# Stage three of a fused attention, gMLP and gated-attention kernel: PSUM handed out by two pools, two moved groups of work, a split gate step and a one-engine last copy

## The chip, the cores and the metric

One core of a Trainium2 chip runs the whole program. The metric is the device time of one execution in microseconds; the kernel before was timed three times. One more execution was taken by the hardware profiler, and all rows below are from that one. TensorE is PE in the rows (its weight loads PEld), VectorE is DVE, ScalarE is ACT, GpSimd is POOL, and SyncE, which issues the transfers, is SP.

## The reference

Four batches of 576 tokens with 512 features go through three stages. Stage one is a pooled plus a local attention, stage two a gMLP block. Stage three, the only one that the change touches, is a mixture of four attention experts with a causal mask, weighted per token by the two largest of four gate logits:

```python
logits = x @ w_gate
topk = np.argpartition(-logits, K, axis=-1)[..., :K]
for e in range(E):
    q = x @ wq[e]; k = x @ wk[e]; v = x @ wv[e]
    scores = np.where(causal, -1e9, scale * (q @ k.transpose(0, 2, 1)))
    a = softmax(scores)
    out += gate_weight[e] * (a @ v @ wo[e])
```

## The kernel before

Stage three works in a fixed order that the program writes out itself; nothing is rescheduled later. Every matmul input of the projections is held as a high and a low part (`split`, L198: ACT copies the high part, DVE subtracts to get the low one), and each product is three matmuls. All PSUM tiles of the stage are single banks from `bank` (L162), eight in turn. A new tile waits until the last reader of the tile that had its bank is done (`reuse_waits="tile"`), also across the border between two pools: the first tiles of stage three wait for readers of the last tiles of stage two, which are the four `f` products that L865 adds to `xT`. Six unused tiles named `past` (L1317) are taken first.

Then `run` (L1321) does nine projections of batch 0: five for values and gate logits (`v`, `jobs_v`) and four for queries and keys of the first two experts (`gq`, `gk`, `proj`, L978). The main loop follows. A step is one of five row blocks (r = 0 to 4, the last shared by two experts) of one expert; a batch has 18 steps. In iteration i the engines get, in the order of the string `STEP = "LSTFaENMd"`: late products (L, among them `av`), the scores of step i (S, PE), the transposes of step i-5 (T, PE), filler jobs planned for this iteration (F), the evacuations of the last iteration's jobs on ACT (a), the exponential of step i-1 (E, ACT), the normalization of step i-2 (N: two small DVE instructions for `sden`, then L1147 on POOL), the masked maximum of step i (M, L1133 on DVE) and the evacuations on DVE (d). Each engine takes its own instructions strictly in that order.

The fillers are planned in L1326 to L1345. `plan` spreads a number of jobs evenly over a span given as first iteration and length:

```python
P1, SPL, PROJ, VJ, OUT = (0, 7), (6, 2), (8, 9), (8, 6), (9, 11)
slots.setdefault(k0 + span[0] + (i * span[1]) // total, []).append(g)
```

`P1` are the four projections of experts 2 and 3 of the batch at work, so in iterations 0, 1, 3, 5. `SPL` are the four splits of the next batch's x (one of four feature blocks each): two in iteration 6, two in 7. `PROJ` and `VJ` start in iteration 8 and need these splits. The gate of a batch (`gate`, L1045) is started by the last `v` job: `gate_rank` is eight DVE instructions (L1066 to L1073) in one evacuation slot, then an exponential on ACT (L1050), then `gate_end` on DVE (L1077 to L1085). The last row tile of the last batch leaves through `last_out` (L1208): two products of 256 columns, each stored by a transfer of its own; ACT copies the first and half of the second, DVE the other half.

Of the kernel before, what the change touches and what calls it, by code (L numbers as in the profile page):

```python
# [8 lines left out]
F32 = mybir.dt.float32  # L9
# [3 lines left out]
AF = mybir.ActivationFunctionType  # L13
# [3 lines left out]
P = 128  # L17
# [78 lines left out]
def tile_pooled_local_attention_gmlp_moe_attention(  # L96
# [18 lines left out]
    act, dve, pool, pe, sp = nc.scalar, nc.vector, nc.gpsimd, nc.tensor, nc.sync  # L115
# [3 lines left out]
    DM = H * D  # L119
# [3 lines left out]
    E = w_gate.shape[1]  # L123
# [21 lines left out]
    NT = 5  # L145
# [4 lines left out]
    px = {}  # L150
# [9 lines left out]
        return px["p"].tile([P, 512], F32, tag="narrow", name=name, bufs=2)  # L160

    def bank(name):  # L162
        return px["p"].tile([P, 512], F32, tag="bank", name=name, bufs=8)

    def psum(name):
        return tc.tile_pool(name=name, bufs=1, space=bass.MemoryType.PSUM, reuse_waits="tile")
# [29 lines left out]
    def split(hi, lo, src, e_hi, e_lo):  # L196
        copy(e_hi, hi, src)
        e_lo.tensor_tensor(lo, src, raw(hi), op=ALU.subtract)  # L198
# [513 lines left out]
    def mm3(o, pairs, first=True, last=True):  # L712
        n = len(pairs)
        for i, (l, r) in enumerate(pairs):
            pe.matmul(o, l, r, start=(first and i == 0), stop=(last and i == n - 1))  # L715

    def three(lh, ll, rh, rl):
        return [(lh, rh), (ll, rh), (lh, rl)]
# [221 lines left out]
    def phase3():  # L940
        with tc.tile_pool(name="m2", bufs=2, reuse_waits="tile") as p:
# [8 lines left out]
            qs, ks, kl, vs, vr, lg, wt, wl = {}, {}, {}, {}, {}, {}, {}, {}  # L950
# [93 lines left out]

            def gate(b):  # L1045
                def rank():
                    l, w, mx = gate_rank(b)

                    def on_act():
                        act.activation(l, l, AF.Exp)  # L1050
                        evac(None, lambda: gate_end(b, l, w, mx))

                    evac(on_act, None)

                evac(None, rank)

            def gate_rank(b):
                l = lg[b]
                sh = [P, NT, E, E]
                a = l[:, :, :, None].to_broadcast(sh)  # L1060
                c = l[:, :, None, :].to_broadcast(sh)
                gt = p.tile(sh, F32, tag="gt", name=f"gt{b}", bufs=1)
                eq = p.tile(sh, F32, tag="eq", name=f"eq{b}", bufs=1)
                w = wt[b] = p.tile([P, NT, E], F32, tag="wt", name=f"wt{b}")
                mx = p.tile([P, NT], F32, tag="gmx", name=f"gmx{b}")
                dve.tensor_tensor(gt, c, a, op=ALU.is_gt)  # L1066
                dve.tensor_tensor(eq, c, a, op=ALU.is_equal)
                dve.tensor_tensor(eq, eq, tri[:, None].to_broadcast(sh), op=ALU.mult)
                dve.tensor_tensor(gt, gt, eq, op=ALU.add)
                dve.tensor_reduce(w, gt, axis=AX.X, op=ALU.add)  # L1070
                dve.tensor_scalar(w, w, 1.5, None, op0=ALU.is_lt)
                dve.tensor_reduce(mx, l, axis=AX.X, op=ALU.max)
                dve.tensor_tensor(l, l, mx[:, :, None].to_broadcast([P, NT, E]), op=ALU.subtract)  # L1073
                return l, w, mx

            def gate_end(b, l, w, mx):
                dve.tensor_tensor(w, w, l, op=ALU.mult)  # L1077
                dve.tensor_reduce(mx, w, axis=AX.X, op=ALU.add)
                dve.tensor_scalar(mx, mx, 1e-9, None, op0=ALU.add)
                dve.reciprocal(mx, mx)  # L1080
                dve.tensor_tensor(w, w, mx[:, :, None].to_broadcast([P, NT, E]), op=ALU.mult)
                t = wl[b] = p.tile([P, 2], F32, tag="wl", name=f"wl{b}")
                for h in range(2):
                    r = slice(64 * h, 64 * h + 64)
                    dve.tensor_copy(t[r], w[r, NQ].rearrange("p (k h) -> p h k", h=2)[:, h])  # L1085
# [3 lines left out]
            def evac(on_act, on_dve):  # L1089
                if on_act:  # L1090
                    pend_act.append(on_act)
                if on_dve:
                    pend_dve.append(on_dve)

            def take(lst):
                got = list(lst)
                lst.clear()
                return got
# [109 lines left out]
            def last_out(b, t, y):  # L1208
                s = p.tile([P, DM], F32, tag="os", name=f"os{b}_{t}", bufs=4)
                os_ = []  # L1210
                for i in range(2):
                    c = slice(i * DM // 2, (i + 1) * DM // 2)
                    o = bank(f"i{b}_{t}_{i}")[:, : DM // 2]
                    os_.append((o, c))
                    mm3(o, [x for kk in range(2)
                            for x in three(y[:, 0, kk], y[:, 1, kk], w2["o"][:, 0, kk, c], w2["o"][:, 1, kk, c])])

                def store(c):
                    sp.dma_start(out=out[b, STARTS[t] : ENDS[t], c], in_=s[:, c])

                (o0, c0), (o1, c1) = os_
                m = DM // 4

                def on_act():
                    act.copy(s[:, c0], o0)
                    store(c0)
                    act.copy(s[:, c1][:, :m], o1[:, :m])

                def on_dve():
                    dve.tensor_copy(s[:, c1][:, m:], o1[:, m:])  # L1230
                    store(c1)

                evac(on_act, on_dve)

            def outp(b, t, kks=(0, 1)):
                if (b, t) == (B - 1, NT - 2):
# [29 lines left out]
            def jobs_split(b):  # L1266
                rem = b % 2 == 0
                if rem:
                    t = xs["rem", b] = cx["p"].tile([P, 2, KT, P], F32R, tag="xrem", name=f"xremb{b}")
                    dst = t.rearrange("p a k (c s) -> p a k c s", c=2)  # L1270
                x = xs[b] = cx["p"].tile([P, 2, KT, S], F32R, tag="xhl", name=f"xhlb{b}")
                for kk in range(KT):
                    split(x[:, 0, kk], x[:, 1, kk], xT[:, b, kk], act, dve)
                    if rem:
                        split(dst[:, 0, kk], dst[:, 1, kk], xT[:, b : b + 2, kk, S - 64 :], pool, pool)
                    yield

            def jobs_proj(b, pr, order=("q0", "q1", "k0", "k1")):
                for nm, hh in order:
                    proj(b, pr, nm, int(hh))  # L1280
                    yield

            def jobs_v(b):
                for t in ([NT - 1] if b % 2 == 0 else []) + list(range(NT - 1)):
                    vproj(b, t)
                    if t == NT - 2:
                        gate(b)
                    yield
# [15 lines left out]
            def drain(fa, fd):  # L1304
                for fn in fa + fd:
                    fn()

            def run(g):
                fa, fd = take(pend_act), take(pend_dve)
                for _ in g:  # L1310
                    drain(fa, fd)
                    fa, fd = take(pend_act), take(pend_dve)
                while fa or fd:
                    drain(fa, fd)
                    fa, fd = take(pend_act), take(pend_dve)

            for i in range(6):  # L1317
                bank(f"past{i}")
            preload = p.tile([P, 1], F32, name="preload", bufs=1)
            act.activation(preload, neghalf, AF.Exp)  # L1320
            first = {"v": jobs_v(0), "p": jobs_proj(0, 0, ("q0", "k0", "q1", "k1"))}  # L1321
            run(next(first[k], None) for k in "vvpvpvvpp")
            steps = [(b, e, r) for b in range(B) for e in range(E) for r in range(NQ + e % 2)]
            NS = E * NQ + 2
            LAG, AVL = 5, 4
            P1, SPL, PROJ, VJ, OUT = (0, 7), (6, 2), (8, 9), (8, 6), (9, 11)  # L1326
            slots = {}

            def plan(k0, span, g, total):
                for i in range(total):  # L1330
                    slots.setdefault(k0 + span[0] + (i * span[1]) // total, []).append(g)

            for b in range(B):
                k0 = b * NS
                plan(k0, P1, jobs_proj(b, 1), 4)
                if b + 1 < B:
                    plan(k0, SPL, jobs_split(b + 1), 4)
                    plan(k0, PROJ, jobs_proj(b + 1, 0), 4)
                    plan(k0, VJ, jobs_v(b + 1), 5 if b % 2 else 4)
                n0 = k0 + NS - NT + LAG  # L1340
                plan(k0 + NS, OUT if b < B - 1 else (LAG + AVL + 1, 5), jobs_out(b), 5 if b % 2 else 4)
            STEP = "LSTFaENMd"
            later = {n0 + r: [lambda r=r: outp(B - 1, r - 2, (0,))] for r in range(2, NT)}
            n = len(steps)
            for i in range(n + LAG + AVL + 8):  # L1345
                fa, fd = take(pend_act), take(pend_dve)
                for k in STEP:
# [13 lines left out]
                    elif 0 <= u < n:  # L1361
                        b, e, r = steps[u]
# [11 lines left out]
        phase2()  # L1374
    px["r"].__exit__(None, None, None)
    cw_pool.__exit__(None, None, None)
    with psum("ps3") as px["p"]:
        phase3()
    cx["c"].__exit__(None, None, None)


# [28 lines left out]
```

## Time and profile before

| what | us |
|---|---|
| median of three runs | 532.11 (531.86 to 532.73) |
| the profiled execution, its own time | 535.39 |
| span of its instructions | 533.6 |
| PE busy in the span | 504.8 (95%) |
| DVE, ACT, POOL busy | 343.6, 269.5, 252.4 |

The span runs from the first instruction to the last; 1.8 us of the profiled execution lie around it. All times in rows are microseconds from the span's start. A row of a timeline gives start, duration, engine, line, operation, output<-inputs and count; in brackets stands the idle time of the engine just before, and what ended it. Neighbouring instructions of one kind are merged into one row, whose duration is that of all of them. Stage three begins at about 348. [...]

### The profile page before, as it was taken

Reading aid. Unit: us, or ns where it says so; the run is one execution under the profiler, and the core shown is the slowest. Engines: PE = TensorE matmul, PEld = TensorE weight load, DVE = VectorE, ACT = ScalarE, POOL = GpSimd, SP = SyncE. Lnnn points to the kernel's source line nnn. Section 1 sums busy time; section 2 is a strip of 40 time slices with the busy share of each in tenths; the row PEclk is TensorE's granted clock in tenths of the full one; section 3 lists DMA queues with packets and bytes.
Section 4 is the critical chain, followed back from the end, with each engine's and each line's share of the span. In section 5 each row is a group of like instructions: output and inputs, shape, how many; then the busy total and the mean of one; then the engine's idle time right before and its main releaser. Section 6 shows DMA issues by size and latency. Waiting matters only on the chain.

```text
span 533.6 us, 12755 instructions
## 1 busy us (share of the span) xinstructions
PE 504.8 (95%) x4955; PEld 459.9 (86%) x4955; DVE 343.6 (64%) x881; ACT 269.5 (50%) x676; POOL 252.4 (47%) x390
## 2 busy tenths in 40 slices
PE   7789878989999999999999999999899999999996
PEld 5677667877989899989998999999888989898885
DVE  4559646886977963743154218438879778868862
ACT  4567655877455343134212322426759557666662
POOL 5769785895532650253024304843436425333540
PEclk9899997999999999999999999999999999999999
DMA  9999999894330102000000000300000010011012
GB/s 185 175 182 186 190 188 181 195 220 75 107 112 2 45 35 61 1 1 0 1 1 0 1 1 11 89 1 2 1 1 1 21 41 21 1 46 55 6 76 98
DMA packets 67811, 34.95 MB, mean 65 GB/s; under 512 B 59176, under 2 KB 60776, under 8 KB 67752
## 3 DMA queue, kind: packets, MB, share of 16 engines
q1 hardware_dynamic: 67752, 34.15, 30.5%
q8 instruction: 39, 0.64, 0.5%
q14 instruction: 20, 0.16, 0.1%
HBM read 29.42 MB, written 4.72 MB: 64 GB/s over the span
## 4 chain that ended last, share of the span: by engine, by line
PE 70%; DVE 8%; POOL 7%; DMA 7%; ACT 2%; SPq 2%; issue 2%; POOLq 0%; DVEq 0%; ACTq 0%
PE f L715 10%; PE e L715 8%; PE du L715 7%; PE dv L715 6%; PE v L715 5%; PE i L715 5%; PE sc L715 5%; PE av L1196 4%; PE gq L715 4%; PE gk L715 4%; DMA v<-in_v_dram 4%; PE tr L1158 3%; DMA vw<-in_v_dram 3%; PE wide L715 2%; PE wide L448 2%
## 5 line engine op out<-in xcount | busy, mean ns | idle before, releaser
L198 POOL TENSOR_TENSOR gT<-z,gT 128x576 fp32r<-128x576 f32 x15 | 23.0, 1539 | 105.3 <-ACT gT L170 105.3
L715 PE MATMUL e<-wsgT,vn 128*128 128x288 f32 x384 | 56.4, 296 | 0.0
L715 PEld LDWEIGHTS e<-wsgT,vn 128*128 128x128 f32 x384 | 53.0, 188 | 0.1
L715 PE MATMUL f<-gT,wouts 128*128 128x288 f32 x384 | 51.8, 295 | 0.0
L715 PEld LDWEIGHTS f<-gT,wouts 128*128 128x128 f32 x384 | 51.4, 188 | 0.0
L170 ACT CAST gT<-z 128x576 fp32r<-128x576 f32 x16 | 10.8, 674 | 78.2 <-DVE z L840 78.2
L715 PE MATMUL dv<-win,xhla 128*128 128x512 f32 x192 | 46.1, 395 | 0.1
L865 DVE TENSOR_TENSOR xT<-f,xT 128x576 f32<-128x576 f32 x16 | 12.1, 758 | 50.5 <-PE f L715 50.5
L715 PEld LDWEIGHTS dv<-win,xhla 128*128 128x128 f32 x192 | 35.5, 188 | 8.1 <-ACT vg L750 0.5
L715 PEld LDWEIGHTS du<-xhla,win 128*128 128x128 f32 x288 | 38.5, 188 | 0.3
L715 PE MATMUL du<-xhla,win 128*128 128x288 f32 x288 | 38.7, 295 | 0.0
L1147 POOL TENSOR_SCALAR xT<-xT,sden,wt 128x128 f32<-128x128 f32 (+3 forms) x32 | 20.5, 641 | 35.9 <-DVE sden L1145 32.5
L1147 POOL TENSOR_SCALAR Xs<-Xs,sden,wt 128x128 f32<-128x128 f32 (+3 forms) x32 | 19.5, 609 | 25.5 <-DVE sden L1145 16.7
L715 PE MATMUL gq<-xhlb,w 128*128 128x288 f32 x192 | 29.7, 301 | 0.1
L715 PE MATMUL gk<-xhlb,w 128*128 128x288 f32 x192 | 29.1, 300 | 0.0
L448 PE MATMUL wide<-aTs,vw 64*64 64x57 f32 (+2 forms) x640 | 22.7, 222 | 5.6 <-DMA vw<-in_v_dram 5.0
L448 PEld LDWEIGHTS wide<-aTs,vw 64*64 64x64 f32 (+1 forms) x640 | 20.8, 137 | 7.7 <-DMA vw<-in_v_dram 4.6
L715 PEld LDWEIGHTS gq<-xhlb,w 128*128 128x128 f32 x192 | 26.2, 189 | 0.6 <-DVE xhlb L198 0.6
L715 PE MATMUL i<-w,yT 128*128 128x512 f32 (+1 forms) x102 | 26.5, 395 | 0.0
L715 PEld LDWEIGHTS gk<-xhlb,w 128*128 128x128 f32 x192 | 26.2, 188 | 0.2
L1133 DVE CUSTOM_DVE_ANT_0 xT<-sc,cmask 128x128 f32<-128x128 f32 (+4 forms) x40 | 19.3, 485 | 10.5 <-PE sc L715 10.1
L1140 ACT ACTIVATE xT<-xT,smx 128x128 f32<-128x128 f32 (+4 forms) x40 | 24.3, 607 | 3.2 <-DVE smx L1133 2.7
(212 smaller groups left out, 1332.2 us busy)
## 6 DMA issues: line engine op xcount, KB each, us to landing
vw<-in_v_dram SPq DMA_DIRECT2D x31, 160.0 KB, 4.3
v<-in_v_dram SPq DMA_DIRECT2D x16, 256.0 KB, 7.4
wst<-in_moe_w_in_dram SPq DMA_DIRECT2D x8, 512.0 KB, 5.7
k<-in_k_dram SPq DMA_DIRECT2D x28, 144.0 KB, 5.4
out_dram<-os SPq DMA_DIRECT2D x15, 256.0 KB, 2.0
q<-in_q_dram SPq DMA_DIRECT2D x22, 144.0 KB, 5.1
wst<-in_moe_w_out_dram SPq DMA_DIRECT2D x4, 512.0 KB, 3.6
q<-in_q_dram SPq DMA_DIRECT2D x5, 288.0 KB, 5.2
```

Of the source, the lines that this page charges most:

```text
L170: act.copy(o, i)
L198: e_lo.tensor_tensor(lo, src, raw(hi), op=ALU.subtract)
L448: pe.matmul(t[64 * h : 64 * h + 64, q0:q1], d["vw"][r, c], aTs[r, c // 2, x0 + q0 : x0 + q1], start=True, stop=True)
L715: pe.matmul(o, l, r, start=(first and i == 0), stop=(last and i == n - 1))
L865: dve.tensor_tensor(dst, os_[mt][:, :, :HS], dst, op=ALU.add)
L1133: dve.tensor_tensor_reduce(out=X[:, c0:c1], in0=os_[i][:, : c1 - c0], in1=tmask if i else cmask[:, z + c0 : z + c1] if r < NQ else cmask[: ...
L1140: act.activation(X, X, AF.Exp, bias=mx, scale=-1.0, accum_out=den)
L1147: pool.tensor_scalar(X, X, den, w, op0=ALU.mult, op1=ALU.mult)
L1158: pe.transpose(o[:, j * P : (j + 1) * P], X[:, s0 : s0 + P], ident)
L1196: pe.matmul(o[64 * h : 64 * h + 64, a0 - c0 : c1 - c0], (vs[b][:, j] if j < NT - 1 else vr[b])[:, e * D : (e + 1) * D], rhs, start=(j == 0 ...
```

## The change

Four things change, all in stage three. `bank` hands out the first two tiles from a tag of their own with two banks and the next from a tag with six, of which one unused tile `past` takes the first; after the nine projections this pool is closed and a second one, with eight banks, serves the rest. `gate_rank` becomes two evacuation steps: `gate_order` (L1066 to L1069) and, one iteration later, the rest (L1070 to L1073). For batch 0, `P1` lies in iterations 0, 1, 2, 3 and `SPL` in 4, 5, 6, 7. `last_out` copies both halves with ACT alone.

```diff
     def bank(name):
-        return px["p"].tile([P, 512], F32, tag="bank", name=name, bufs=8)
+        px["n"] = px.get("n", 8) + 1
+        if px["n"] < 2:
+            return px["p"].tile([P, 512], F32, tag="narrow", name=name, bufs=2)
+        return px["p"].tile([P, 512], F32, tag="bank", name=name, bufs=6 if px["p"] is px.get("first") else 8)
...
             def gate(b):
                 def rank():
-                    l, w, mx = gate_rank(b)
-
-                    def on_act():
-                        act.activation(l, l, AF.Exp)
-                        evac(None, lambda: gate_end(b, l, w, mx))
-
-                    evac(on_act, None)
+                    gt = gate_order(b)
+
+                    def count():
+                        l, w, mx = gate_rank(b, gt)
+
+                        def on_act():
+                            act.activation(l, l, AF.Exp)
+                            evac(None, lambda: gate_end(b, l, w, mx))
+
+                        evac(on_act, None)
+
+                    evac(None, count)
 
                 evac(None, rank)
...
-                (o0, c0), (o1, c1) = os_
-                m = DM // 4
-
                 def on_act():
-                    act.copy(s[:, c0], o0)
-                    store(c0)
-                    act.copy(s[:, c1][:, :m], o1[:, :m])
-
-                def on_dve():
-                    dve.tensor_copy(s[:, c1][:, m:], o1[:, m:])
-                    store(c1)
-
-                evac(on_act, on_dve)
+                    for o, c in os_:
+                        act.copy(s[:, c], o)
+                        store(c)
+
+                evac(on_act, None)
...
-            for i in range(6):
-                bank(f"past{i}")
+            px["n"] = -1
+            px["first"] = px["p"]
+            px["p"].tile([P, 512], F32, tag="bank", name="past", bufs=6)
             preload = p.tile([P, 1], F32, name="preload", bufs=1)
             act.activation(preload, neghalf, AF.Exp)
             first = {"v": jobs_v(0), "p": jobs_proj(0, 0, ("q0", "k0", "q1", "k1"))}
             run(next(first[k], None) for k in "vvpvpvvpp")
+            px["ps"].__exit__(None, None, None)
+            px["ps"] = psum("ps4")
+            px["p"] = px["ps"].__enter__()
...
-                plan(k0, P1, jobs_proj(b, 1), 4)
+                plan(k0, P1 if b else (0, 5), jobs_proj(b, 1), 4)
                 if b + 1 < B:
-                    plan(k0, SPL, jobs_split(b + 1), 4)
+                    plan(k0, SPL if b else (4, 4), jobs_split(b + 1), 4)
```

## Rows read from the trace of the kernel before

**Rows 1.** Stretches: start:end, length, busy time and count by engine, PEclk, DMA, GB/s.

```profile
347.80:348.70 0.90, 0.07 (x1) 0.00 (x0) 0.80 (x2) 0.00 (x0) 0.69 (x2) 1.00 0.00 0
362.50:377.40 14.90, 13.43 (x95) 12.13 (x93) 13.49 (x49) 10.80 (x29) 7.44 (x15) 1.00 0.01 2
377.40:389.30 11.90, 11.90 (x96) 11.73 (x97) 8.45 (x37) 7.94 (x23) 5.82 (x11) 1.00 0.01 1
...
417.30:529.60 112.30, 112.21 (x817) 98.70 (x816) 81.97 (x331) 68.10 (x194) 40.66 (x78) 1.00 0.11 39
```

**Rows 2.** Timeline of the border between stage two and stage three.

```profile
348.72 0.42 PEld L715 LDWEIGHTS v<-w,xremb 128*128 128x128 f32 x3 [1.08 <-DVE xT L865]
```

**Rows 3.** The chain that ended last, in order of time: where it leaves DVE.

```profile
363.41 0.45 DVE kl L1005
...
376.66 0.66 PE gq L715 x3
```

**Rows 4.** Timelines of DVE and, last row, of ACT around batch 0's gate.

```profile
361.13 0.24 DVE L1070 TENSOR_REDUCE wt<-gt 128x20 f32<-128x80 f32 x1
...
361.90 0.94 DVE L1005 TENSOR_TENSOR qs<-gq,qs 64x288 fp32r<-64x288 f32 x2
363.41 0.94 DVE L1005 TENSOR_TENSOR kl<-gk,ks 64x288 fp32r<-64x288 f32 x2 [0.57 <-ACT ks L1000]
...
365.83 0.29 DVE L1133 CUSTOM_DVE_ANT_0 xT<-sc,cmask 128x128 f32<-128x128 f32 x1
...
360.98 0.80 ACT L1000 CAST qs<-gq 64x288 fp32r<-64x288 f32 x2 [1.21 <-PE gq L715]
```

**Rows 5.** Timeline of DVE in iterations 5 to 7 of batch 0.

```profile
371.83 0.15 DVE L1144 TENSOR_SCALAR sden<-sden 128x1 f32<-128x1 f32 x1
...
372.56 1.42 DVE L198 TENSOR_TENSOR xhlb<-xT,xhlb 128x576 fp32r<-128x576 f32 x2
...
374.16 0.54 DVE L1133 CUSTOM_DVE_ANT_0 Xs<-sc,cmask 128x384 f32<-128x384 f32 x1
...
374.83 0.91 DVE L1005 TENSOR_TENSOR kl<-gk,ks 64x288 fp32r<-64x288 f32 x2
...
375.77 1.50 DVE L198 TENSOR_TENSOR xhlb<-xT,xhlb 128x576 fp32r<-128x576 f32 x2
```

**Rows 6.** Timeline of PE at the end of the same stretch.

```profile
374.85 0.63 PE L1158 MATMUL tr<-ident,xT 128*128 128x128 f32 x4 [1.35 <-DVE smx L1133]
...
377.56 1.60 PE L715 MATMUL v<-w,xhlb 128*128 128x260 f32 x12
```

**Rows 7.** Timeline of POOL: the normalization of 512 columns, twice.

```profile
372.73 1.81 POOL L1147 TENSOR_SCALAR xT<-xT,sden,wt 128x512 f32<-128x512 f32 x1
...
380.49 0.77 POOL L1147 TENSOR_SCALAR Xs<-Xs,sden,wt 128x512 f32<-128x512 f32 x1 [1.13 <-DVE sden L1145]
```

**Rows 8.** Timelines of DVE, then of PE, around batch 1's gate.

```profile
392.64 0.42 DVE L1133 CUSTOM_DVE_ANT_0 Xs<-sc,cmask 128x256 f32<-128x256 f32 x1
...
397.83 0.82 DVE L1200 TENSOR_TENSOR yT<-av,yT 128x256 fp32r<-128x256 f32 x2
...
393.22 0.52 PE L1158 MATMUL tr<-ident,xT 128*128 128x128 f32 x3 [0.50 <-DVE smx L1133]
...
398.36 0.91 PE L715 MATMUL gq<-xhlb,w 128*128 128x288 f32 x5
```

**Rows 9.** Everything that DVE waited for from 389.3 to 420.6: total, times, longest.

```profile
DVE Xs L1133 <- PE sc L715: 2.2, 1, 2.2
```

**Rows 10.** Timeline of the last copies and transfers.

```profile
528.86 1.11 SPq L1259 DMA_DIRECT2D out_dram<-os  x2
...
529.55 0.27 ACT L1227 COPY os<-i 128x128 f32<-128x128 f32 x1 [0.33 <-PE i L715]
529.85 0.29 DVE L1230 COPY os<-i 128x128 f32<-128x128 f32 x1 [1.02 <-ACT os L1227]
530.06 1.02 SPq L1219 DMA_DIRECT2D out_dram<-os  x2
```

More of the change, by code (lines that the diff above doesn't have):

```diff
@@ L1046, in rank, with gate_order @@
                 def rank():
-                    l, w, mx = gate_rank(b)
-                    def on_act():
-                        act.activation(l, l, AF.Exp)
-                        evac(None, lambda: gate_end(b, l, w, mx))
-                    evac(on_act, None)
+                    gt = gate_order(b)
[6 more added lines that the diff above has]
+                    evac(None, count)
                 evac(None, rank)
-            def gate_rank(b):
+            def gate_order(b):
                 l = lg[b]
@@ L1063, in gate_rank @@
                 eq = p.tile(sh, F32, tag="eq", name=f"eq{b}", bufs=1)
-                w = wt[b] = p.tile([P, NT, E], F32, tag="wt", name=f"wt{b}")
-                mx = p.tile([P, NT], F32, tag="gmx", name=f"gmx{b}")
                 dve.tensor_tensor(gt, c, a, op=ALU.is_gt)
@@ L1069, in gate_rank @@
                 dve.tensor_tensor(gt, gt, eq, op=ALU.add)
+                return gt
+            def gate_rank(b, gt):
+                l = lg[b]
+                w = wt[b] = p.tile([P, NT, E], F32, tag="wt", name=f"wt{b}")
+                mx = p.tile([P, NT], F32, tag="gmx", name=f"gmx{b}")
                 dve.tensor_reduce(w, gt, axis=AX.X, op=ALU.add)
@@ L1376, in tile_pooled_local_attention_gmlp_moe_attention @@
     cw_pool.__exit__(None, None, None)
-    with psum("ps3") as px["p"]:
-        phase3()
+    px["ps"] = psum("ps3")
+    px["p"] = px["ps"].__enter__()
+    phase3()
+    px["ps"].__exit__(None, None, None)
     cx["c"].__exit__(None, None, None)
```

## The prediction, made before the changed kernel was run

> **What bounds the kernel now.** I read the windows first, by stage, for who is busy where; then what PE waits for; then the chain, to see where it leaves PE; then timelines at those places. From 348.7 to the last product PE is the bound: it is busy all the time but for three holes, all before 398 (from 417.3 on 112.2 of 112.3 us are busy [rows 1]), and only these can be won.
>
> Hole one is the border of the stages: 0.90 us in which PE does next to nothing [rows 1]. The first `v` product starts at 348.72, and the last addition L865 is named as what it waited for [rows 2]. Its operands don't come from there; it is the PSUM bank of the last `f` tile that `v` was given.
>
> Hole two is in batch 0's iterations 0 to 7. From 362.5 to 377.4 DVE is busy 13.5 of 14.9 us, more than PE [rows 1], and the chain goes from PE to DVE with the `kl` subtraction at 363.41 and comes back at 376.66 with the first `gq` of batch 1 [rows 3]. There PE stands 1.35 us before the transpose at 374.85, and the following `gq` group takes until `v` starts at 377.56 [rows 6].
>
> Hole three is 0.50 us before the transpose at 393.22, which waits for the maximum L1133 that stands behind batch 1's gate on DVE [rows 8].
>
> **First bank.** The first two `v` products would get the tag of two banks. In stage two the tag of the wide tiles is named first and that of two banks (`narrow`, for the `dv` products) after it; here `past` is named first and the two-bank tag after it, with the same sizes. So the two should lie where stage two's `narrow` lay, and the `dv` tiles were read long before. Then `v` starts when the last `f` product is issued. Hole one gives back 348.72 - 347.80 = 0.92 us by the windows, and about 0.1 more because the first weight load then hides behind `f`: 1.0 us. The bounds are 0 (the bank still waits) and 1.08, the idle time of the weight load [rows 2]. I take 1.0. Nothing else is late: everything up to 362 on ACT, DVE and POOL follows PE's products. The gain lasts, because the chain up to 363 is PE's, and DVE's long stretch starts with what PE gives it.
>
> **Closing the pool** adds no instruction. If the new pool gives first a bank whose evacuation is late (`kl`, ending at 363.41 + 0.94 = 364.35), one projection starts up to 1.9 us late; PE has that much idle time before 374.85, so what is left of it on DVE I put at 0 to 0.5. I take 0, as with eight banks in order of release the late ones come last.
>
> **Gate of batch 0.** Before, DVE did the eight instructions in one go and had 0.57 us of idle time before `kl` [rows 4]. After, the last four (361.13 to 361.90, 0.77 us) stand behind the `qs` pair. That pair must wait until ACT's two casts end at 360.98 + 0.80 = 361.78, so DVE idles there instead; then 361.81 + 0.96 + 0.77 = 363.54 against 363.41: `kl` and all behind it start 0.13 us later. The first maximum moves from 365.83 to about 365.97.
>
> **Projections and splits.** DVE is the bound of this stretch, and ahead of the fourth split stand the same DVE instructions in both kernels: four pairs of `qs`/`kl`, seven maxima, five small norms, the copy of a transpose, three splits. Their order alone changes, so the fourth split can't end before the present 377.27 (375.77 + 1.50) plus 0.13 [rows 5]. What changes is what comes early. The normalization of step 3 needs its `sden`, now at 371.83. In the new order the last `kl` pair (0.91) and two splits (1.42) come ahead of it, so 371.83 + 2.33 + 0.13 = 374.3; some 0.5 us later POOL starts, 0.77 us long when alone [rows 7]: 375.6. The transpose that needs it waits now until 374.85, for a bank by the row; it would move to 375.6 at the earliest. The bank for batch 1's first `gq`, seven tiles behind the scores of step 6, should be the one that the maximum of step 6 frees, now at 374.16 + 0.54 = 374.70 [rows 5]; with `kl` (0.91), the third split (0.72) and 0.13 ahead of it that is 376.4. Then twelve products run without holes; their group lasts 1.6 where nothing is late (the `v` row, of as many products, shows 1.60 [rows 6]). So `v` starts at 376.45 + 1.6 = 378.05 instead of 377.56: 0.5 us lost. PE's idle time moves and grows; it isn't filled.
>
> Contention can make it worse. The same normalization took 1.81 us at 372.73, while the two splits at 372.56 ran, and 0.77 at 380.49 [rows 7]. In the new order it starts at about 374.8 and the third split at 374.9. With part of that 1.04 us the transpose comes at 376.2 and `v` at 378.2. I take 0.55 us lost in all.
>
> [...]
>
> The bounds of this part: a loss of 2.3 us if the norm were held until 0.56 us after the fourth split, as it ended 0.56 us after the second now (373.98 and 374.54); a gain of at most 0.3, if splits ran without contention and nothing else were late. More is excluded by the unchanged set of instructions. After 377.4 PE is the bound again with DVE at 8.45 of 11.9 us [rows 1], so what is lost stays lost.
>
> **Gate of batch 1.** The maximum at 392.64 would come 0.77 us earlier, since four instructions move behind it, and the hole of 0.50 closes. But from 389.3 to 420.6 DVE waits only once, for the first scores in that stretch [rows 9]. In that stretch PE starts `gq` at 398.36, about when the first of two subtractions of 0.41 us from 397.83 ends (398.24) [rows 8], and it reads the bank that `gq` needs. The same DVE instructions stand ahead of it in both orders, so PE gets there sooner and waits there. I take 0.05 us of gain, bounds 0 and 0.50. In batches 2 and 3 PE has no hole at the gate: 0.
>
> **Last tile.** DVE's copy ends at 529.85 + 0.29 = 530.14; ACT alone would do 256 columns in about 0.37 us, twice 128 columns less one start, so 529.92. But the last transfer is issued by SP, which has two other transfers until 529.97 and then issues the first half from 530.06; the second half follows in the middle of 1.02 us, at about 530.6 [rows 10]. The data waits for the queue either way: 0, bounds 0 and 0.22.
>
> **Sum.** -1.0 + 0.55 - 0.05 + 0 = -0.5 us. The profiled execution would go from 535.39 to 534.9. It lies 3.28 us over the median of the three runs, a constant for this purpose, so the same difference is taken off the median: 531.6 us, 0.1% less.
>
> **Rivals.** A measurement of this kernel tells 0.2%, 1.06 us, from no change.
>
> *PE keeps its lead.* Banks come free in another order under the new pool, so that neither the `gq` at 376.4 nor the one at 398.36 waits for DVE, the splits cost nothing, the gate's hole is won and the tail's 0.22 too: -1.0 - 0.50 - 0.22 = -1.7 us, 530.4; with the 0.3 that the splits could gain, 530.1. For it: the transpose at 374.85 waited for a bank, so banks do bind, and each of the parts takes work off a place where PE stands. Against it: DVE's set of instructions is unchanged and has no hole. I give it 0.37, with all that lies below 531.05.
>
> *The early splits hold up the norm.* Place: POOL's norm of step 3 between the second and the fourth split. Price: the upper bound of 2.3 us, so -1.0 + 2.3 - 0.05 = +1.25, 533.4. It decides if that norm ends after 377. For it: 1.81 us at 372.73. Against it: between the later splits DVE does other work in which POOL ran at its usual time. 0.08.
>
> *The first bank still waits*, because the two-bank tag lies elsewhere than I think: the start gains nothing, +0.5, 532.6. Place and proof: the first `v` behind L865. 0.08; it counts as no change.
>
> **Chances.** Forecast 0.47, likeliest and within 0.2% like the third rival: same 0.55. Faster 0.37, slower 0.08. The forecast's own range is 531.0 to 532.2. The whole range takes in the first rival and the third, 530.1 to 532.8, and leaves out the second.
>
> **What the profile after would show.** Right: the first `v` right behind `f` with no wait for L865; the norm of 512 columns of step 3 on POOL near 1 us later, counted from the first `v`, and the transpose after it; the wait before the gate's transpose gone and a new one near the `gq` that followed 398; the last transfer issued as long after the first half's as before. Wrong: `v` of batch 1 no later, counted from the first `v`, than the 377.56 - 348.72 = 28.84 us now (then order, not the sum, set DVE's stretch), or PE's lead still there at the `gq`.

## The result and the profile after

The changed kernel takes 535.46 us (median of four runs, 534.45 to 535.57) against 532.18 us for the kernel before (its three runs and one more): 3.28 us more. The ratio, here and below, is formed from all runs and not from the two medians; it is 1.0056, with a 95% interval of 1.0039 to 1.0074. The prediction was 531.6.

The two profiled executions differ before stage three begins: the last `f` product starts at 347.58 in before and at 344.17 in after. So the measure used from here on is **the stretch**, from the start of that last `f` product to the end of the span. It is 186.06 us in before and 189.68 us in after, 3.62 us more. `v` of batch 1 comes 33.50 us after the first `v`, against 28.84. From there to the end both take as long (156.04 us in after, 156.07 in before), so whatever is lost is lost before that point.

The border, in a timeline of after with PE's weight load and first product (start, duration, idle time before and its end in brackets):

```profile
344.18 0.92 PEld L718 LDWEIGHTS v<-w,xremb 128*128 128x128 f32 x7
344.31 0.88 PE L718 MATMUL v<-w,xremb 128*128 128x260 f32 x6
```

The wait of 1.08 us for the last addition [rows 2] is gone. 0.13 us after the last `f` product started, `v` starts; in before it was 1.14 us.

The scores of step 0 and what follows, in timelines of PE and then of DVE:

```profile
360.29 0.30 PE L718 MATMUL sc<-ks,qs 128*128 128x128 f32 x1 [2.25 <-DVE kl L1008]
...
360.54 2.31 PE L718 MATMUL gq<-xhlb,w 128*128 128x288 f32 x12
...
363.07 2.62 PE L718 MATMUL gq<-xhlb,w 128*128 128x288 f32 x12
...
357.32 0.94 DVE L1008 TENSOR_TENSOR qs<-gq,qs 64x288 fp32r<-64x288 f32 x2 [0.72 <-ACT qs L1003]
...
359.22 0.92 DVE L1008 TENSOR_TENSOR kl<-gk,ks 64x288 fp32r<-64x288 f32 x2
...
363.31 0.42 DVE L1145 CUSTOM_DVE_ANT_0 xT<-sc,cmask 128x256 f32<-128x256 f32 x1 [1.40 <-PE sc L718]
```

This wait is new. The scores read keys and queries that were ready long before; what they wait for is the `kl` pair of `gk0_0_1`, the last tile of the first pool. In the program as built the first tile of the second pool, these scores, lies in the very bank of that tile (bank 0; the tiles behind it get the banks 7, 6, 1, 5, 2, 3 and 4). In before the same scores lie in the bank of the second `v` tile and do not wait. Then DVE, which I took to be the bound from here on, itself waits 1.40 us for scores.

The windows show that the wait is not all (start:end, length, busy time and count of PE, PEld, DVE, ACT, POOL, then PEclk, DMA share, GB/s):

```profile
343.40:344.30 0.90, 0.90 (x9) 0.90 (x8) 0.00 (x0) 0.00 (x0) 0.00 (x0) 1.00 0.08 18
357.90:360.30 2.40, 0.15 (x3) 0.04 (x1) 2.22 (x8) 1.00 (x3) 1.34 (x4) 1.00 0.01 3
360.30:362.40 2.10, 2.10 (x13) 2.10 (x14) 1.39 (x9) 0.00 (x0) 0.00 (x0) 0.81 0.04 8
362.40:365.00 2.60, 2.60 (x13) 2.60 (x13) 1.58 (x6) 1.28 (x4) 0.00 (x0) 0.50 0.00 0
```

PE does next to nothing for 2.4 us, starts at full clock (PEclk 1.00), and 1.3 us later the granted clock falls to 0.50 for 3.4 us (361.6 to 365.0): products of 288 columns come 240 ns apart, against 133 at full clock.

The rest of the stretch up to `v` of batch 1, in timelines of PE, POOL and DVE:

```profile
374.72 0.66 PE L1170 MATMUL tr<-ident,xT 128*128 128x128 f32 x4 [0.73 <-POOL xT L1159]
376.13 1.83 PE L718 MATMUL gq<-xhlb,w 128*128 128x288 f32 x12 [0.76 <-DVE smx L1145]
...
373.90 0.77 POOL L1159 TENSOR_SCALAR xT<-xT,sden,wt 128x512 f32<-128x512 f32 x1 [0.17 <-POOL ks L180]
...
374.07 1.19 DVE L201 TENSOR_TENSOR xhlb<-xT,xhlb 128x576 fp32r<-128x576 f32 x1
```

The norm of 512 columns takes 0.77 us where it took 1.81 [rows 7], and the split beside it 1.19 where two took 1.42 [rows 5]. The transpose now waits for that norm, and the `gq` for the maximum, as the prediction had it.

Last, the two other places, in timelines of PE at batch 1's gate and of ACT and SP at the end:

```profile
398.41 1.06 PE L718 MATMUL gq<-xhlb,w 128*128 128x288 f32 x6 [0.25 <-DVE yT L1212]
...
529.67 0.37 ACT L1235 COPY os<-i 128x256 f32<-128x256 f32 x1 [0.34 <-PE i L718]
530.17 1.03 SPq L1231 DMA_DIRECT2D out_dram<-os  x2
```

The hole before the gate's transpose [rows 8] is gone and a wait stands at the next `gq`. The last copy ends at 530.04, and SP issues the two last transfers from 530.17 on, in 1.03 us as before.

### The profile page after: what moved, and what is told of

Its sections match the earlier page's. It is cut to its first block, busy times and chain, and to the rows that moved or that the text cites. A ratio compares the mean times of both kernels' runs of the same rounds, so it can differ in the third digit from the quotient of the medians.

```text
span 533.8 us, 12750 instructions
## 1 busy us (share of the span) xinstructions
PE 506.1 (95%) x4955; PEld 460.9 (86%) x4955; DVE 343.3 (64%) x880; ACT 269.5 (50%) x676; POOL 251.7 (47%) x390
## 4 chain that ended last, share of the span: by engine, by line
PE 72%; DMA 9%; DVE 8%; POOL 5%; ACT 3%; issue 2%; SPq 1%; POOLq 0%; DVEq 0%; ACTq 0%
PE f L718 10%; PE e L718 8%; PE du L718 7%; PE dv L718 6%; PE gq L718 5%; PE v L718 5%; PE i L718 5%; PE sc L718 5%; PE gk L718 4%; PE av L1208 4%; PE tr L1170 3%; DMA v<-in_v_dram 3%; DMA q<-in_q_dram 3%; PE wide L718 2%; DMA vw<-in_v_dram 2%; PE wide L451 2%
## 5 line engine op out<-in xcount | busy, mean ns | idle before, releaser
L718 PEld LDWEIGHTS gq<-xhlb,w 128*128 128x128 f32 x192 | 27.5, 198 | 1.4 <-ACT aT L173 1.0
L718 PE MATMUL v<-w,xhlb 128*128 128x260 f32 x192 | 25.7, 283 | 0.0
```

## The experiments

Two theories: **A**, the loss is the late bank and the fall of the clock behind it; **B**, the moved projections and splits cost it on DVE. The stretch tells kernels apart far better than the timed runs: for a kernel profiled twice with the same clock it agrees within 0.05 us, while the 23 or 35 runs of before beside the experiments spread over 5 to 7 us, and the last `f` of the profiles starts anywhere from 343.71 to 349.34. The kernels from "fills alone" on in the table were profiled once each; in all of these profiles the clock is full from the last `f` to the last product.

| kernel | stretch, us | against before |
|---|---|---|
| before | 186.06 | |
| after: three profiles | 189.68, 188.16, 189.71 | +3.62, +2.10, +3.65 |
| after, idle time filled: two profiles | 188.19, 188.14 | +2.13, +2.08 |
| after, other bank: two profiles | 188.03, 186.43 | +1.97, +0.37 |
| pools alone: two profiles | 186.06, 186.04 | 0.00, -0.02 |
| pools alone, other bank: two profiles | 184.97, 184.99 | -1.09, -1.07 |
| fills alone | 187.35 | +1.29 |
| projections alone, splits alone | 186.31, 187.78 | +0.25, +1.72 |
| gate alone | 186.31 | +0.25 |
| after, other bank, fills as before | 185.28 | -0.78 |

**The bank.** The eighth tile, `gq0_0_1`, takes a third tile of the two-bank tag; `gk0_0_1` then gets another bank, which the second pool gives out as sixth.

```diff
-        if px["n"] < 2:
+        if px["n"] < 2 or px["n"] == 7:
```

> The kernel after, but the last gq tile of the first pool (gq0_0_1) takes a third tile of the two-bank tag, so that gk0_0_1 no longer lies in the bank that the second pool gives first to the scores of step 0. Theory A (the whole loss is the bank: 2.4 us of idle PE at the scores of step 0, and about 2 us more because the granted clock falls behind it): the scores start right behind gk, the clock stays at 1.00, and the time is what the other parts leave, 531.2 to 532.2 us against 532.2 before. Theory B (the early projections and splits of batch 0 cost it on DVE): the wait goes, but the loss appears later as waits of PE for DVE between 363 and 376, and the time stays over 534.5.

The wait at the scores was gone, and yet the median was 535.85 us against 533.23; the runs lie so far apart (529.66 to 537.25) that the ratio of 1.0014 (0.9977 to 1.0050) tells no difference. The profile, of an execution of 535.88 us, shows what happened in it. A row of PE, then windows:

```profile
371.09 0.55 PE L1170 MATMUL tr<-ident,xT 128*128 128x128 f32 x3 [1.83 <-POOL xT L1159]
```

```profile
368.50:370.30 1.80, 0.76 (x5) 0.31 (x3) 1.71 (x6) 1.75 (x5) 0.72 (x2) 1.00 0.02 5
370.30:371.50 1.20, 0.41 (x4) 0.41 (x5) 1.16 (x5) 1.20 (x4) 1.05 (x2) 1.00 0.00 0
...
376.00:377.00 1.00, 1.00 (x6) 1.00 (x6) 0.97 (x6) 0.53 (x1) 0.68 (x2) 0.50 0.00 0
```

PE, early now, stands 1.83 us before the transposes of step 2 (for POOL's norm), and here the clock falls, from 371.7 to 378.5. So neither theory as put held. A's wait was real, but its time was missed, since the fall can come behind another wait. B's signs were there (a median over 534.5 and later waits of PE between 363 and 376), but in this profile part of the loss is the clock. The same kernel again:

> The kernel after with gq0_0_1 in the two-bank tag, once more; the first time the clock fell at 371.7 and the stretch from the last f to the end was 188.03. If the parts add up (pools without their wait -1.09, fills +1.29, gate +0.25, tail about 0) and the clock stays up: 186.3 to 186.7. If they cost more together: 187 or more with the clock up. With a fall: about 188 again.

The clock stayed up and the stretch was 186.43, as the sum of the parts said. So in the whole change the late bank costs 188.16 - 186.43 = 1.73 us, and a fall here 1.60.

**The clock.** 18 products into a tile that nobody reads stand where PE idled:

```diff
+            dm = px["p"].tile([P, 512], F32, tag="narrow", name="dm", bufs=2)
+            mm3(dm[:, :HS], [(w2["qk"][:, 0, 0, :P], xs[0][:, 0, 0, :HS])] * 18)
             px["ps"].__exit__(None, None, None)
```

> The kernel after, with 18 products more between the last gk and the end of the first pool, into a tile that nobody reads: 18 x 133 ns = 2.4 us of work just where PE stood idle. The scores of step 0 start at the same moment as in after. Theory A with the clock as half of it: the granted clock stays at 1.00 behind the scores, the following gq products come 133 ns apart instead of 240, and the time falls by 1 to 2 us, to 533.5 to 534.5. Rival (the fall of the clock is hidden behind DVE's work or has another cause): the time stays at 535.5, or the clock falls all the same.

The median was 534.96 us, a little over the 533.5 to 534.5 expected; the ratio to before is 1.0032 (1.0000 to 1.0065). The windows of this kernel, to be laid beside those of after:

```profile
357.80:360.20 2.40, 2.40 (x20) 2.36 (x18) 2.22 (x8) 1.01 (x3) 1.35 (x4) 1.00 0.00 0
360.20:362.30 2.10, 2.10 (x18) 2.07 (x17) 1.47 (x9) 0.00 (x0) 0.00 (x0) 1.00 0.05 12
362.30:365.00 2.70, 2.70 (x23) 2.70 (x22) 2.14 (x7) 2.07 (x6) 0.30 (x1) 1.00 0.00 0
```

The clock stays up, and the stretch is 1.49 us shorter than after's. But one profile each does not show that the idle time brings the fall, so after itself was run again:

> The kernel after, unchanged, profiled once more on this chip, to see whether the granted clock falls each time behind the 2.4 us of idle PE. If the idle stretch alone decides: the fall recurs at the same place and the stretch from the last f to the end is 189.5 to 189.9 again. If it does not always follow: the wait is there and the clock stays at 1.00, 188.0 to 188.4 as in the run with busy products.

> The kernel after, a third profile and more timed runs. The wait at the scores of step 0 is there each time (2.4 us). From the last f to the end: 189.5 to 189.9 with a fall of the clock, 188.0 to 188.4 without. If the fall hangs on the idle stretch it is seen in about half of the executions, as in one of two so far; the timed median stays 2 to 3.5 us over before.

> The kernel after with 18 products in the idle stretch, once more. If the idle stretch brings the fall, the clock stays at 1.00 behind the scores again, 188.0 to 188.4 from the last f to the end. A fall at the same place with no idle time before it would speak for another cause.

The second profile of after had the wait and no fall. Its PE row and its windows:

```profile
360.50 0.30 PE L718 MATMUL sc<-ks,qs 128*128 128x128 f32 x1 [2.25 <-DVE kl L1008]
```

```profile
358.20:360.50 2.30, 0.05 (x1) 0.03 (x1) 2.12 (x8) 1.00 (x3) 1.27 (x4) 1.00 0.01 4
360.50:362.60 2.10, 2.10 (x16) 2.10 (x17) 1.41 (x9) 0.00 (x1) 0.00 (x0) 1.00 0.03 8
```

The third had the fall again, at the same place (a mean of 0.54 from 361.40 to 365.10), and its timed runs repeat the first result: 536.80 against 533.64, ratio 1.0054 (1.0033 to 1.0074). The filled kernel had none in two. So the wait of 2.25 us was followed by the fall in two of three executions, and a fall costs after 189.68 - 188.16 = 1.52 us.

**The pools alone**, as in after, and with the other bank:

> The kernel before, with the two pools as in after (two-bank tag for the first two tiles, closed after the nine projections) and nothing else. Theory A: the scores of step 0 wait for the same bank, PE idles some 2.3 us and the clock falls, against 1.0 won at the border: +2.5 to +3.5 us, 534.7 to 535.7. Theory B: the pools alone gain, 531.0 to 532.0.

> The pools of after alone, once more: the wait of 2.3 us is there, and the clock may fall behind it. Without a fall 186.0 to 186.2 from the last f to the end, with one 187.3 to 187.8.

> The kernel before, with the two pools of after but gq0_0_1 in the two-bank tag (so that the scores of step 0 do not meet the bank of gk0_0_1), and no other part of the change. From the last f to the end, 186.06 in before and in the pools alone. Theory A (the pools alone lost at the scores of step 0 what they won at the border): no wait at the scores, 1.0 us won, 185.0 to 185.2; with a fall of the clock 1.5 to 2 more. Rival (PE's lead is lost at the next bank or behind DVE): 185.8 to 186.1.

> The pools with gq0_0_1 in the two-bank tag and nothing else, once more: 184.9 to 185.1 from the last f to the end, and 1.1 us (0.2%) under before in the timed runs, if the earlier stages do not hide it; the rival, that the first profile was a lucky one, gives 185.8 or more.

With the late bank, the scores wait 1.95 us and the clock stays up both times; the border's gain is lost to 0.02 us, and the median of 534.12 stands at 1.0007 (0.9983 to 1.0031). Theory A's +2.5 to +3.5 was a miss: it had counted the whole wait and a fall. Theory B's gain was a miss too. The row of the scores:

```profile
362.69 0.30 PE L718 MATMUL sc<-ks,qs 128*128 128x128 f32 x1 [1.95 <-DVE kl L1008]
```

With the other bank the gain stays: -1.09 and -1.07. Border and scores of that kernel:

```profile
344.96 0.88 PE L718 MATMUL v<-w,xremb 128*128 128x260 f32 x6
...
358.52 0.22 PE L718 MATMUL sc<-ks,qs 128*128 128x128 f32 x1
```

So the wait of 1.95 us costs 1.09, since PE's later waits take up part of it: the one before the transposes of step 3 is 1.35 us with the other bank and 0.61 with the late one. In the whole change the wait is 0.30 us longer, because the gate's last four instructions stand ahead of that `kl` pair, and the later waits again take up about 0.75 us; what else makes 1.73 out of 1.09 was not taken apart.

The pools with the other bank are the best version, by the stretch. Their timed runs don't tell them from before: 0.9999 (0.9973 to 1.0025) and 0.9985 (0.9958 to 1.0012).

**The fills, whole and in halves.** Each takes one or both changed `plan` lines into before.

> The kernel before, with batch 0's projections and splits planned as in after and nothing else. Theory A: what my sum gave this part, +0.3 to +0.8 us, so 532.5 to 533.0. Theory B: it carries the loss, +3 us and more, 535 or more.

> The kernel before, with only batch 0's projections of experts 2 and 3 planned in iterations 0 to 3; the splits stay in 6 and 7. Fills as a whole: 187.35 from the last f to the end against 186.06. Theory C (the third split, moved between the norm's divisor and the maximum of step 6, is held up by POOL's norm and so delays the bank for batch 1's first gq; the projections cost little): 186.0 to 186.4. Rival (the last kl pair, 0.91 us on DVE, now ahead of the norms, is the loss): 186.9 or more.

> The kernel before, with only batch 0's splits planned one by one in iterations 4 to 7; the projections stay in 0, 1, 3 and 5. Theory C: the splits carry most of the 1.29, 186.7 to 187.3 from the last f to the end, and one split near POOL's norm of 512 columns takes 1.1 to 1.3 us instead of 0.7. Rival (the projections carry it): 186.0 to 186.4.

1.29 us for both (timed 1.0013, 0.9985 to 1.0041), 0.25 for the projections, 1.72 for the splits. With both, in timelines of DVE, POOL and PE:

```profile
372.65 1.20 DVE L198 TENSOR_TENSOR xhlb<-xT,xhlb 128x576 fp32r<-128x576 f32 x1
...
372.48 0.77 POOL L1147 TENSOR_SCALAR xT<-xT,sden,wt 128x512 f32<-128x512 f32 x1 [0.17 <-POOL ks L177]
...
374.72 1.83 PE L715 MATMUL gq<-xhlb,w 128*128 128x288 f32 x12 [0.77 <-DVE smx L1133]
```

With the projections alone, in timelines of DVE and POOL:

```profile
372.50 1.42 DVE L198 TENSOR_TENSOR xhlb<-xT,xhlb 128x576 fp32r<-128x576 f32 x2
...
372.55 1.93 POOL L1147 TENSOR_SCALAR xT<-xT,sden,wt 128x512 f32<-128x512 f32 x1
```

In these rows whichever starts first keeps its time, and the other is stretched: the norm, 0.17 us ahead, takes 0.77 and the split 1.20; the splits, 0.05 ahead, take 1.42 for both and the norm 1.93. In after the norm is first, again by 0.17, and the split beside it, of 1.19 us, stands before the maximum that frees the bank of `gq`.

The splits alone have a second loss, in timelines of ACT and DVE:

```profile
370.02 0.67 ACT L170 CAST xhlb<-xT 128x576 fp32r<-128x576 f32 x1 [1.63 <-PE gk L715]
...
370.72 0.76 DVE L198 TENSOR_TENSOR xhlb<-xT,xhlb 128x576 fp32r<-128x576 f32 x1 [0.99 <-ACT xhlb L170]
```

The parts of the next x go into the one buffer from which the last `gk` still reads, so the first split cannot run until the projections are done. The two moves belong together. Theory C was right on the projections and on the stretched split (1.20 us here too); its size for the splits was too low, as it did not have this wait.

**The gate, and all but the fills.** The gate's two steps in before, and after with the other bank and the old plan:

> The kernel before, with the gate in two evacuation steps as in after and nothing else. Measured as the stretch from the start of the last f product to the end of the span, 186.06 in before. By my sum (+0.13 on DVE in batch 0, -0.05 at batch 1's gate) 185.9 to 186.2. Rival: the gate is what is missing between after without its fall of the clock (188.19 in the run with busy products) and the fills and the pools alone (+1.29 and 0.00), so +0.8: 186.7 or more.

> The kernel after with gq0_0_1 in the two-bank tag and with batch 0's projections and splits planned as before. Theory A (the fills are the other loss, the gate and the tail cost nothing): 184.8 to 185.3 from the last f to the end, about 1 us under before. Rival (gate or tail cost): 185.8 or more.

The gate costs 0.25, between the two expectations. Timeline of DVE there:

```profile
360.16 0.94 DVE L1005 TENSOR_TENSOR qs<-gq,qs 64x288 fp32r<-64x288 f32 x2 [0.72 <-ACT qs L1000]
...
361.69 0.34 DVE L1082 TENSOR_TENSOR lg<-lg,gmx 128x20 f32<-128x20 f32 x1
362.07 0.94 DVE L1005 TENSOR_TENSOR kl<-gk,ks 64x288 fp32r<-64x288 f32 x2
```

`kl` starts 15.03 us after the first `v` (347.04), against 363.41 - 348.72 = 14.69: 0.34 later. What the gate of batch 1 gives back is 0.09. The last tile by ACT alone is what remains: 185.28 - (184.97 + 0.25) = 0.06. The ends of the profiles say the same: from the start of the last product to the end of the span it takes 4.40 to 4.44 us in the nine profiles with the old copies and 4.46 to 4.51 in the eight with ACT alone; the cause of this difference was not sought. The timed runs of this version stand at 1.0007 (0.9977 to 1.0036).

## Why the prediction was wrong

The measured steps lead from before to after: pools with an early bank -1.09; fills, gate and tail on top of them 186.43 - 184.97 = +1.46; the late bank +1.73; the fall of the clock +1.52. Together 189.68; the steps are taken one on top of the other, so they add up by construction. The prediction's sum was -0.5.

- **First bank** (-1.0): right, -1.09 and -1.07, and 1.14 - 0.13 = 1.01 at the border itself.
- **Closing the pool** (0, bounds 0 to 0.5): the step that failed, and twice. Its condition, that the new pool gives a late bank first, was written down with the right instruction, `kl`; then I took it as not the case, since "in order of release the late ones come last". The first tile got the latest bank of all. And its price was wrong: I let PE's later idle time pay for a wait of 1.9 us, but the row named has only 1.35 [rows 6], and 0.74 of it paid. The late tile was not one of a projection but that of the scores, for which DVE's maxima wait, so DVE, the bound behind, was held up too (0.70 us before the second maximum with the pools alone). The price is 1.09 us with the pools alone and 1.73 in the whole change. It could have been settled without a run: the order of the banks follows from the program.
- **The clock** stood in no step, and its fall costs 1.52 us. In before it is full through stage three (PEclk 1.00 from 348.6 to 529.6), and I let each hole of PE cost its own length.
- **Projections and splits** (+0.55 with the gate's 0.13): right in kind, too small. With the fills alone the norm came 26.14 us after the first `v`, where I had 374.8 - 348.72 = 26.08. But I took the contention on the norm, and only part of it; the norm was first, and the split took 0.45 us longer than the 0.75 of one alone. By the rows `v` was to come at 378.05 to 378.2; with the fills alone it came 30.05 us after the first `v`, which is 378.77 in before's time. Fills alone cost 1.29.
- **Gate of batch 0** (+0.13): 0.34 for `kl`. The wait for ACT's casts was as described; the last of the four instructions, ahead of `kl`, took 0.34 us where it took 0.18 in before, and I had 0.77 for all four where 0.94 pass until `kl` starts. In after it took 0.34 as well (at 358.85), and a copy of `ks` on POOL had started 0.11 us ahead of it (358.74); in before none ran beside it. **Gate of batch 1** (-0.05): right, 0.09, with the new wait at the `gq`.
- **Last tile** (0): right within 0.06, but a loss, which the bounds of 0 and 0.22 of gain left out.
- The rivals: none was it. "Early splits hold up the norm" gave slower, but with the roles exchanged and a chance of 0.08; no rival had a late bank, though its place and instruction were in the text. That is what the chance of slower lacked.

## What to carry to other kernels

When a PSUM pool is closed and another opened, look up which bank its first tile gets and who reads that bank last; the work of a program's border should not meet the youngest tile of the pool before. Price a wait by what stands behind the waiting tile on the other engines, not by the waiting engine's idle time later. Of a split on DVE and a norm on POOL that fall together, the one that started first kept its time here (the norm 0.77 us, two splits 1.42) and the other was stretched (a split to 1.19 or 1.20 us, the norm to 1.81 or 1.93), so a step that is moved also decides which of the two is stretched.

## What was not expected of the hardware

The granted clock. Behind 2.25 us of waiting at full clock it fell to 0.50 in two of three profiles of the same program, a little over 1 us after PE had started again, and came back while PE was busy all the time (in the first profile 1.3 us after, and back at 365.0). Behind waits of 1.83 to 1.95 us it fell in one of four profiles (the pools alone twice, the other bank twice). With the wait of 2.25 us filled with products it fell in neither of two. The other stages of the same traces bear this out. In before the clock falls at 21.2 and 82.6, behind waits of PE of 3.00 us (until 19.20) and 3.94 (until 81.60), and stays at 1.00 behind one of 2.31 (until 36.35); in after it falls at 78.3, behind 2.67 us (until 78.14). Up to the last product the 17 profiles show 36 falls to 0.50, and each comes during or just behind a wait of PE, the shortest of them 1.57 us long; none comes within unbroken work. Of their 39 waits of 2 us or more 34 had such a fall and five had none, the longest of these 2.81 us. So idle time goes ahead of the fall every time in these profiles; why the fall comes in one execution and not in the next stays open. In the first timed runs of after, three lie at 535.42 to 535.57 and one at 534.45; whether the one is without a fall was not seen.
